# Transposing three units early, storing u in the output, and moving the weight-part stores to SyncE in a fused attention and MLP-mixer kernel

## The chip, the cores and the metric

The kernel runs on one core of one Trainium2 chip. The metric is device time in microseconds (us), the median of several runs; lower is better. Besides, one execution was taken by the hardware profiler; all durations of single instructions come from it. The engines are PE (TensorE, matrix products), DVE (VectorE), ACT (ScalarE), POOL (GpSimd) and SP (SyncE, which here only issues DMA transfers).

## The reference

All in float32. Eight batches of 576 tokens, 8 heads of 64, model width 512. First linear attention with a normalisation, then a token mixing (over the 576 tokens), then a channel mixing (over the 512 columns, hidden width 1536):

```python
kv = np.einsum('bhsd,bhse->bhde', k, v)
out = np.einsum('bhsd,bhde->bhse', q, kv)
rms = np.sqrt(np.mean(out * out, axis=-1, keepdims=True) + 1e-06)
x = out / rms * g_norm                      # then (B,H,S,D) -> (B, S, H*D)
h = np.maximum(x.transpose(0, 2, 1) @ w_tok1, 0.0) @ w_tok2
u = x + h.transpose(0, 2, 1)
h2 = np.maximum(u @ w_ch1, 0.0) @ w_ch2
return u + h2
```

## The kernel before

**First pass (0 to about 195 us).** Batches go in four pairs. For each pair `attention` computes kv, the attention output, its norm and x, and `token_mixing` turns x into u. The work of a pair's mixing is interleaved with the attention of the next pair by lists of step names that `play` reads word by word (`start`, `middle`, `steady`, `last`). Each name is a closure: "h00" a product of token mixing, "u3" the second product of tile 3, "g", "q", "t" parts of the norm, "f3" a load of a raw block of channel weights, a number so many steps of rounding those weights. x and u share the tiles `X[pair, i]`; two sets of them (`xps`) take turns, so that pair 2 overwrites pair 0. `tok2` stores u in DRAM from POOL's queue (lines 565 to 569).

**Units.** The channel mixing sees u as nine units of 512 tokens: unit b is the first 512 tokens of batch b, unit 8 collects the last 64 tokens of all eight batches. Each unit has a DRAM tile `u_dram[u]` (line 108). Unit 0 is group 0; the rest are groups 1 to 4 of two units, 1024 tokens (`units`, line 579).

**Transposing.** The channel mixing needs u with columns on partitions. `fetch_t(u, i)` loads 128 tokens (256 KB) into a buffer xt; `turn_blocks(u, i)` has DVE transpose blocks of 32 x 32 from xt into a buffer y (two instructions), and after each second tile issues four DMAs that write y to a DRAM tile `blocks_dram`. `fetch_half`, through `fetch_once` and `fetch_u`, loads these blocks into uT in full transposed order. All those DMAs are in SP's queue, which issues in program order.

**Products by Strassen-like schemes.** Both products of the channel mixing are done with seven block products in place of eight, at two levels (outer blocks o, inner parts n), so sums of weight blocks, of u and of v are needed. The sums of the weights are made once: `split(weight, o)` makes one outer block's parts and stores seven of them in DRAM (`parts_dram`). Parts of the first weight are stored by SP (`queue`, line 285), and two of the sums are made on POOL; parts of the second weight are stored by ACT's queue (`nc.scalar`), with DVE making all sums. Each split has five stores for the second weight, 35 for seven blocks. In `second` weight's case the sums lie in free halves of v tiles.

**The stage of group 0 (about 195 to 297 us).** `channel1_once` and `channel2_once` give the seven products of group 0 with whole weights in SBUF; `weave` distributes a list of other steps between them: sums (`firsts`, `lasts`), `parts1`, `parts2`, the loads and transposes of units 1 and 2 (`turn_unit`), the loads of uT of group 1 and of its first weight parts (lines 1299 to 1325).

**The groups 1 to 4 (from about 283 us, 138 us a group).** `channel1(g, n0)` and `channel2(g, n0)` put their products on numbered places, seven to an outer block, 49 to a layer; `put(place, step)` puts any other step behind the product of that place. A last loop emits products and steps place by place. A place takes PE about 1.34 us. `fetch_ahead` loads weight parts one block ahead; lines 980 to 985 place the transposes of the next group's units at places 2, 5, 9, 12, 49, 52, 76 and 80 with the load of each next tile one place behind; xt and y have one buffer each there (lines 1311, 1312). `outer_u` and `inner_u` make sums of u: the sum of block 4 takes, at place 10 of each group, one of three buffers "us". These buffers also hold results of the previous group's channel2, which POOL adds into the output with accumulating DMAs (`join`, line 1090); before that SP has copied u from `u_dram` to the output inside DRAM (line 1096). Group 4 instead has u in SBUF (`xg`, loaded by `fetch_x`), adds results there with DVE (`xadd`) and stores from it. Lines 1077 to 1086 place the sums of v (`ins`, `S1` to `S4`) in channel2.

Of the kernel before, what the change touches and what calls it, by code (L numbers as in the profile page):

```python
# [20 lines left out]
def kernel(  # L21
# [32 lines left out]
    nc = tc.nc  # L54
# [52 lines left out]
    kvp = [inp.tile([P, HP, P], F32, name=f"kvp{i}") for i in range(2)]  # L107
    u_dram = [dram.tile([J * P, DM], F32, name=f"u_dram{g}") for g in range(NU)]

# [8 lines left out]
    def dma(o, i, engine=nc.sync):  # L118
        keep(engine.dma_start(o, i))  # L119
# [160 lines left out]
    def split(weight, o):  # L280
# [3 lines left out]
        to = parts_dram[weight, o]  # L284
        queue, other = (nc.sync, nc.gpsimd) if weight == 1 else (nc.scalar, nc.vector)

# [230 lines left out]
    def token_mixing(pair, seeds, aside=()):  # L517
# [26 lines left out]
        def tok2(i):  # L544
# [19 lines left out]
            if i == 8:  # L564
                dma(u_dram[B][ts(pair, P)], x, nc.gpsimd)
            elif i % 2 == 1:
                dma(
                    u_dram[2 * pair + i // J][ds((i % J - 1) * P, 2 * P)]
                    .rearrange("(t p) e -> p t e", p=P), X[pair, i // 2], nc.gpsimd)
# [12 lines left out]
    def fetch_x(g, i):  # L582

        if g < NG:
            if i == 0:
                xg[g] = (late["xg"].tile([P, 2 * J, DM], F32, name="xg") if g else
                         late["xg0"].tile([P, J, DM], F32, name="xg"))
            dma(xg[g][:, ts(i, J)], u_dram[units(g)[i]].rearrange("(t p) e -> p t e", p=P))

    def fetch_t(u, i):  # L590

        if u < NU:
            xt[u, i] = late["xt"].tile([P, DM], F32, name="xt")
            dma(xt[u, i], u_dram[u][ts(i, P)])

    Q = 32
    blocks, blocks_dram = {}, {}

    def turn_blocks(u, i):
        if u >= NU:  # L600
            return
        half, n = i // 2, 2 * (i % 2)
        if n == 0:
            blocks[u] = late["y"].tile([P, NC, 2, NC, Q], F32, name="y")
        for o in range(2):
            keep(nc.vector.transpose(  # L606
                blocks[u][:, :, o, n:n + 2].rearrange("p b n t -> p n b t"),
                xt[u, i][:, ts(o, DH)].rearrange("p (n b t) -> p n b t", n=2, b=NC)))
        if n:
            t = blocks_dram[u, half] = dram.tile([NC, Q, NC, 2 * P], F32, name=f"blocks{u}{half}")  # L610
            for a in range(NC):
                dma(t[:, :, a].rearrange("b i x -> i b x"),
                    blocks[u][ds(a * Q, Q)].rearrange("p b o n t -> p b (o n t)"))

# [319 lines left out]
    def channel1(g, n0):  # L934
# [40 lines left out]
        for t, *places in ((2, None, 24, 28, 26), (7, 45, 46, 47, 48), (1, None, 44, 47, 46)):  # L975
            for place, (i, j) in zip(places, ((0, 0), (0, 1), (1, 0), (1, 1))):
                if place is None:
                    continue
                rectify(place, t, i, j)
        for k, place in enumerate((2, 5, 9, 12, 49, 52, 76, 80)):  # L980
            u = units(g + 1)[k // J]
            put(b + place, do(turn_blocks, u, k % J))
            if k < 7:
                put(b + place + 1, do(fetch_t, units(g + 1)[(k + 1) // J], (k + 1) % J))
        put(b + 84, do(fetch_t, units(g + 2)[0], 0))
        for place, step in zip((-2, 1, -1, 10), outer_u(g)):
# [3 lines left out]
    def channel2(g, n0):  # L990
# [86 lines left out]
        for place, steps in (  # L1077
                (-3, [ins[1][0]]), (-1, [ins[1][1]]), (1, [ins[1][3]]), (2, [ins[1][2]]),
                (3, [ins[2][0]]), (5, [ins[2][1]]), (6, [ins[4][0]]), (7, [ins[2][2]]),
                (8, [A[0]]), (9, [A[1]]), (10, [ins[2][3]]), (11, [S3[0]]), (12, [S3[1]]),  # L1080
                (13, [ins[4][1]]), (14, [ins[4][2]]), (15, [S2[0]]), (16, [ins[4][3]]), (17, [ins[7][0]]), (18, [xadd(0, 0, 1)] if g == NG - 1 else []),
                (19, [ins[7][1]]), (21, [S2[1], ins[7][2]]), (23, [ins[7][3]]), (24, [S1[0]]),
                (25, [ins[6][0]]), (29, [S4[0]]), (27, [ins[6][1]]), (28, [S1[1]]), (30, [ins[6][2]]),
                (31, [ins[5][0], ins[6][3]]), (33, [ins[5][1]]), (34, [xadd(0, 0, 2)] if g == NG - 1 else []),
                (35, [ins[5][2]]), (36, [S4[1]]), (37, [ins[5][3]]), (39, [ins[3][0]]), (41, [ins[3][1]]),
                (43, [ins[3][2]]), (45, [ins[3][3]])):
            put(b + place, *steps)

        if g < NG - 1:
# [4 lines left out]

            for i in range(2):
                put(b - 6 + 3 * i, do(lambda i: dma(out[units(g)[i], :LO], u_dram[units(g)[i]]), i))
            for place, step in ((12, join(0, 0, 1)), (20, join(0, 0, 2)), (26, join(1, 0, 4)), (40, join(0, 1, 6)),
# [6 lines left out]
        else:  # L1104
            for place, steps in ((36, [do(store_part, 0, 0, J, 0)]),
                                 (40, [xadd(1, 0, 4)]), (43, [xadd(0, 1, 6)]), (44, [radd(7, 6)]),
                                 (45, [xadd(1, 0, 7)]), (45, [xadd(0, 1, 5)]), (46, [xadd(1, 1, 7)]),
                                 (47, [xadd(1, 1, 5), do(store, g, 1)]),
                                 (48, [do(store_part, 0, 0, 2, 1)]), (49, [do(store_part, 0, 2, 4, 1)])):
                put(b + place, *steps)  # L1110
# [82 lines left out]
    for block in tok1[2:] + tok2:  # L1193
# [19 lines left out]
    steady = [[  # L1213
        "kv00 kv01 e00 e01 1 -d40 f3", "h00 1", "h01 1 f4", "a0 q00 g01 q01 g00 l00 1",
        "h10 t00 t01 1", "h11 l01 1", "hr 1 z2 f5 f6", "a1 q10 g11 q11 g10", "kv10 kv11 e10 e11 t10 t11 m0 r0",
        "u0 i0 1", "u1 1 d00 l10", "u2 s01 z4 1 f7", "a2 q20 g21 q21 g20", "u3 s10 t20 t21",
        "u4 z6 1 l11", "a4 q40 g41 q41 g40 lq0", "u5 d11 t40 t41 1", "a3 q30 g31 q31 g30 lq1",
        "u6 t30 t31 m2 r2 i2 d20 p21 s30", "u7 1 d31 1", "u8 1"], [
        "kv00 kv01 e00 e01 1 -d40 f8", "h00 1", "h01 1 f9", "a0 q00 g01 q01 g00",
        "h10 t00 t01 1", "h11 1", "hr 1 z2 f10", "a1 q10 g11 q11 g10", "kv10 kv11 e10 e11 t10 t11 m0 r0",  # L1220
        "u0 i0 1", "u1 1 d00 f11", "u2 s01 z4 1", "a2 q20 g21 q21 g20", "u3 s10 t20 t21",
# [8 lines left out]
    more = {f"w{n}{k}": f for n, b in enumerate(tok1 + tok2) for k, f in enumerate(b)}  # L1230
    more |= {f"f{n}": b[0] for n, b in enumerate(channel)}
    rounding = stream(channel)

# [18 lines left out]
    late["u0"] = pool("u0", 1, "left", once)  # L1252
    late["xt"] = pool("xt0", 2, "left", once)
    late["y"] = pool("y0", 2, "left", once)
    fetch_t(0, 0)
    fetch_t(0, 1)
    fill = [list(rounding), mix_ch1()]
    woven = fill[0][:4] + fill[1] + fill[0][4:]

    def turn(i):  # L1260
        turn_blocks(0, i)
        if i + 2 < J:
            fetch_t(0, i + 2)
        if i % 2:
            fetch_once(i // 2)

    last = [
        "h00 c0 2 -d40 2", "h01 c1 2", "h10 c2 2", "h11 c3 2", "hr z2 1", "u0 z3 1", "u1 z4 1", "u2 z5",
        "u3 z6 1", "u4 z7 1", "u5 z8 1", "u6 1", "u7 c4", "u8"]
    more = {f"c{i}": do(turn, i) for i in range(J)}  # L1270
    more[f"c{J}"] = lambda: [f() for f in t_sums(lambda n: uT[0][:, SB[n]])]
    woven = iter(woven)
# [7 lines left out]
    late["xg0"] = pool("xg0", 1, "right", w2s)  # L1280
    late["sv0"] = pool("sva", 2, "right", tail)
    late["r0"] = pool("r0", 5, "right", tail)
# [4 lines left out]
    firsts, lasts = mix_ch2()  # L1287
    parts1 = [f for o in ORDER1 for f in split(1, o)]
    parts2 = [f for o in ORDER2 for f in split(2, o)]

    def turn_unit(u):
        steps = [do(fetch_t, u, 0)]
        for i in range(J):
            steps.append(do(turn_blocks, u, i))
            if i + 1 < J:
                steps.append(do(fetch_t, u, i + 1))
        return steps

    fill, turns = firsts + parts1, turn_unit(1)
    for i, f in enumerate(turns):  # L1300
        fill.insert(5 * i, f)
    weave(channel1_once(0), fill)
    tail.close()
# [6 lines left out]
    late["ui"] = pool("ui", 2)  # L1310
    late["xt"] = pool("xt", 1)
    late["y"] = pool("y", 1)
    late["tmp"] = pool("tmp", 1)
    late["us"] = pool("us", 3)
    turns = turn_unit(2)
    waits = [[do(fetch_u, 1, 0, h) for h in range(2)]] + [[f] for f in lasts[:2]] + [turns[:1]] + [[f] for f in lasts[2:]]
    for i in range(J):
        waits += [turns[2 * i + 1:2 * i + 3]] + [[f] for f in parts2[2 * i:2 * i + 2]]
        if i < 2:
            waits += [[do(fetch_w, 0, 2 * i), do(fetch_w, 0, 2 * i + 1)]]  # L1320
    waits += [[f] for f in parts2[8:16]] + [[do(fetch_u, 1, 1, 0), do(fetch_w, 1, 0)]]
    waits += [[f] for f in inner_u(1, 1)] + [[do(fetch_u, 1, 1, 1), do(fetch_w, 1, 1)]]
    waits += [[f] for f in parts2[16:]] + [[do(fetch_t, units(2)[0], 0)]] + [[f] for f in outer_u(1)[:1]]
    waits += [[lambda: staged[-1]()], outer_u(1)[2:3]]
# [57 lines left out]
```

## Time and profile before

| What | Value |
|---|---|
| median of 3 runs | 861.64 us (861.49 to 863.35) |
| the profiled execution, whole | 857.33 us |
| its span, first to last instruction | 855.5 us |
| mean granted PE clock | 0.973 |
| DMA moved | 205.22 MB, mean 240 GB/s |
| SP's queue (q1) | 103840 packets, 169.31 MB |
| POOL's queue (q0) | 16880 packets, 23.60 MB |
| ACT's queue (q10) | 12096 packets, 11.37 MB |
| xt loads | 36 of 256 KB, median 4.1 us from issue to landing |
| block writes (y to blocks) | 72 of 128 KB, median 2.5 us |
| transposes on DVE | 72, mean 422 ns |
| accumulating stores | 27 of 512 KB, median 9.9 us (from r) and 8.1 us (from us) |

A profile line that begins with a start and a duration is one instruction, or a merged run of equal ones (x12: twelve records; one product of the program leaves two). What stands in brackets at its end is the idle time of the engine before it and what ended it. SPq and ACTq are DMA issues. "PE ps_d <- ACT ps_d" in a list of waits reads: PE, about to write ps_d, waited for ACT's last work on it.

### The profile page before, as it was taken

How to read it: one execution, taken by the hardware profiler on the slowest of the kernel's cores; microseconds unless marked ns; L12 is line 12 of the kernel's file. 1: busy time of each engine (PE TensorE's matmuls, PEld its weight loads, DVE VectorE, ACT ScalarE, POOL GpSimd, SP SyncE). 2: the span in 40 equal slices, each digit the busy share in tenths (PEclk: the TensorE clock that was granted, in tenths of full speed). 3: DMA queues.
4: the chain of work that ended last, by engine and by line, in shares of the span. 5: the costliest groups of instructions: out<-in, count | busy, mean ns of one | idle time of the engine just before them, and what ended most of it. 6: DMA issues, size and time to landing. Idle time of an engine off the chain costs nothing.

```text
span 855.5 us, 14847 instructions
## 1 busy us (share of the span) xinstructions
PE 792.4 (93%) x5832; PEld 661.3 (77%) x5832; DVE 609.9 (71%) x901; ACT 265.2 (31%) x513; POOL 79.2 (9%) x86
## 2 busy tenths in 40 slices
PE   6999999999994499999998999998999999899995
PEld 6655545447883388899987899897889998789995
DVE  3667585996756558988647889755898863788885
ACT  2366474842100033421132252022342113224110
POOL 1302020202500000001210001020000121000000
PEclk9999999999997799999999999999999999999997
DMA  9999994566998976789897589799679899655542
GB/s 303 315 342 334 343 377 152 195 211 201 345 287 271 381 219 189 245 248 248 219 249 229 148 281 293 210 226 253 188 248 258 235 223 277 206 149 154 143 126 74
DMA packets 132884, 205.22 MB, mean 240 GB/s; under 512 B 9712, under 2 KB 89584, under 8 KB 132720
## 3 DMA queue, kind: packets, MB, share of 16 engines
q1 hardware_dynamic: 103840, 169.31, 62.4%
q0 software_dynamic: 16880, 23.60, 13.9%
q10 hardware_dynamic: 12096, 11.37, 4.1%
q8 instruction: 46, 0.75, 0.4%
q14 instruction: 22, 0.18, 0.1%
HBM read 148.80 MB, written 61.73 MB: 246 GB/s over the span
## 4 chain that ended last, share of the span: by engine, by line
PE 66%; DMA 14%; DVE 11%; issue 4%; ACT 3%; SPq 2%; POOL 1%; DVEq 0%; ACTq 0%; POOLq 0%
PE ps_d L131 21%; PE ps_b L131 13%; PE ps_a L131 13%; PE ps_h L131 7%; DMA xt<-u_dram 7%; PE ps_u L131 6%; DVE v L122 3%; PE ps_kv L131 2%; SPq L119 2%; PE ps_o L131 2%; DMA out_dram<-r 2%; DVE sv L122 2%; PE ps_c L131 1%; DVE y L606 1%; ACT x L486 1%
## 5 line engine op out<-in xcount | busy, mean ns | idle before, releaser
L131 PE MATMUL ps_d<-ui,w 128*128 128x256 f32 x504 | 124.9, 394 | 16.3 <-ACT ps_d L128 11.9
L131 PEld LDWEIGHTS ps_d<-ui,w 128*128 128x128 f32 x504 | 98.6, 198 | 32.8 <-ACT ps_d L128 12.3
L128 ACT COPY ps_d<-ps_a 128x768 f32<-128x768 f32 (+1 forms) x56 | 32.0, 571 | 247.2 <-PE ps_a L131 190.4
L122 DVE TENSOR_TENSOR v<-v,v 128x1536 f32<-128x1536 f32 (+2 forms) x70 | 103.0, 1476 | 0.3
L131 PE MATMUL ps_b<-w,sv 128*128 128x128 f32 x672 | 87.4, 281 | 7.6 <-DVE sv L122 7.6
L131 PEld LDWEIGHTS ps_b<-w,sv 128*128 128x128 f32 x672 | 81.8, 197 | 8.6 <-DVE sv L122 8.4
L131 PE MATMUL ps_a<-w,v 128*128 128x128 f32 x672 | 84.2, 275 | 0.0
L131 PEld LDWEIGHTS ps_a<-w,v 128*128 128x128 f32 x672 | 79.9, 192 | 0.2
L131 PE MATMUL ps_d<-w,v 128*128 128x128 f32 x528 | 67.6, 279 | 2.7 <-DVE xg L122 2.7
L131 PE MATMUL ps_u<-h,w_tok 128*128 128x512 f32 (+1 forms) x160 | 67.5, 607 | 0.2
L131 PEld LDWEIGHTS ps_d<-w,v 128*128 128x128 f32 x528 | 64.2, 196 | 3.0 <-DVE xg L122 2.9
L606 DVE STREAM_TRANSPOSE y<-xt 128x256 f32<-128x256 f32 x72 | 27.6, 422 | 53.6 <-DMA xt<-u_dram 52.6
L131 PE MATMUL ps_h<-x,w_tok 128*128 128x512 f32 (+1 forms) x160 | 65.5, 603 | 0.2 <-ACT x L486 0.2
L125 ACT ACTIVATE v<-v 128x768 f32<-128x768 f32 (+1 forms) x54 | 42.6, 822 | 68.3 <-DVE v L122 65.9
L131 PE MATMUL ps_d<-w,sv 128*128 128x128 f32 x480 | 60.1, 275 | 0.0
L131 PEld LDWEIGHTS ps_d<-w,sv 128*128 128x128 f32 x480 | 57.1, 192 | 0.2
L1092 POOL DMA_DIRECT2D out_dram<-us x12 | 15.4, 1281 | 386.6 <-ACT us L128 278.4
L131 PEld LDWEIGHTS ps_h<-x,w_tok 128*128 128x128 f32 (+1 forms) x160 | 26.1, 189 | 32.2 <-issue 27.7
L131 PEld LDWEIGHTS ps_u<-h,w_tok 128*128 128x128 f32 (+1 forms) x160 | 24.7, 179 | 31.3 <-issue 25.4
L131 PE MATMUL ps_a<-uT,w 128*128 128x256 f32 x192 | 47.5, 384 | 0.4
L131 PE MATMUL ps_b<-ui,w 128*128 128x256 f32 x168 | 41.9, 386 | 6.3 <-DVE v L122 6.3
L432 DVE TENSOR_TENSOR x<-ps_o,g_sb 128x512 f32<-128x512 f32 x32 | 21.5, 687 | 33.8 <-PE ps_o L131 29.2
(141 smaller groups left out, 1224.0 us busy)
## 6 DMA issues: line engine op xcount, KB each, us to landing
w<-parts SPq DMA_DIRECT2D x168, 384.0 KB, 4.1
w<-parts SPq DMA_DIRECT2D x56, 192.0 KB, 3.6
qT<-in_q_dram SPq DMA_DIRECT2D x8, 1152.0 KB, 9.2
xt<-u_dram SPq DMA_DIRECT2D x36, 256.0 KB, 4.1
blocks<-y SPq DMA_DIRECT2D x72, 128.0 KB, 2.5
uT<-blocks SPq DMA_DIRECT2D x36, 256.0 KB, 5.6
k_in<-in_k_dram SPq DMA_DIRECT2D x16, 512.0 KB, 9.0
u_dram<-x POOLq DMA_DIRECT2D x16, 512.0 KB, 5.7
```

The lines of the kernel that those rows point to most:

```text
L119: keep(engine.dma_start(o, i))
L122: keep(engine.tensor_tensor(out=o, in0=a, in1=b, op=op))
L125: keep(nc.scalar.activation(o, a, AF.Relu))
L128: keep(nc.scalar.copy(o, a))
L131: keep(nc.tensor.matmul(*a, **kw))
L432: keep(nc.vector.tensor_mul(x, bank[c, h], g_sb.to_broadcast([P, number(c), D])))
L486: keep(nc.scalar.activation(x[:, k, h], x[:, k, h], AF.Copy, scale=inv[:, k, h]))
L606: keep(nc.vector.transpose(blocks[u][:, :, o, n:n + 2].rearrange("p b n t -> p n b t"), xt[u, i][:, ts(o, DH)].rearrange("p (n b t) -> p n ...
L1092: return lambda: keep(nc.gpsimd.dma_start(out[u, :LO, ts(j, DH)].rearrange("(t p) e -> p t e", p=P), rs[o][0], accum_op=ALU.add))
```

## The change

It has six parts.

1. Units 0, 1 and 2 are transposed in the first pass, right from X, by `turn_early` at the names "x00" to "x21" in the two `steady` lists. The space for y is a part of `w_ch2` that has not been filled yet. No xt load is needed. The list `last` loses its transposes ("c0" to "c3" are now sums of u) and gets the first five steps of `parts1` ("s0" to "s4"); the pool for these sums has four buffers, not two.
2. In `split` the second weight's parts are stored by SP.
3. u is stored in the output itself; only unit 8 has a DRAM tile of its own, `u_rest`. The six copies inside DRAM go.
4. In the groups the transposes are at places 2, 6, 10, 14, 17, 20, 23 and 26; xt has two buffers, and loads run two tiles ahead, the first two of the next group's at places 60 and 66.
5. In channel2 the order of the sums for blocks 6 and 5 is changed at places 30 to 38.
6. In group 4 the additions into xg are at other places, mostly earlier.

PE's instructions and their order are the same. DVE's stream has the same instructions in another order. ACT's stream loses 35 DMA issues.

```diff
-    u_dram = [dram.tile([J * P, DM], F32, name=f"u_dram{g}") for g in range(NU)]
+    u_rest = dram.tile([J * P, DM], F32, name="u_rest")
+    u_rows = lambda u: u_rest if u == B else out[u, :LO]
...
-        queue, other = (nc.sync, nc.gpsimd) if weight == 1 else (nc.scalar, nc.vector)
+        queue, other = (nc.sync, nc.gpsimd if weight == 1 else nc.vector)
...
-                    u_dram[2 * pair + i // J][ds((i % J - 1) * P, 2 * P)]
+                    u_rows(2 * pair + i // J)[ds((i % J - 1) * P, 2 * P)]
...
+    def turn_tile(y, x, i):
+        for o in range(2):
+            keep(nc.vector.transpose(
+                y[:, :, o, 2 * i:2 * i + 2].rearrange("p b n t -> p n b t"),
+                x[:, ts(o, DH)].rearrange("p (n b t) -> p n b t", n=2, b=NC)))
+
+    def put_blocks(u, half, y):
+        t = blocks_dram[u, half] = dram.tile([NC, Q, NC, 2 * P], F32, name=f"blocks{u}{half}")
+        for a in range(NC):
+            dma(t[:, :, a].rearrange("b i x -> i b x"),
+                y[ds(a * Q, Q)].rearrange("p b o n t -> p b (o n t)"))
...
+    def turn_early(u, half):
+        pair, c = u // 2, 2 * (u % 2) + half
+        y = w_ch2[:, c if pair == 0 else 2 + c, :NC].rearrange("p b (o n t) -> p b o n t", o=2, n=NC)
+        for i in range(2):
+            turn_tile(y, X[pair, c][:, i], i)
+        put_blocks(u, half, y)
...
-        for k, place in enumerate((2, 5, 9, 12, 49, 52, 76, 80)):
+        for k, place in enumerate((2, 6, 10, 14, 17, 20, 23, 26)):
             u = units(g + 1)[k // J]
             put(b + place, do(turn_blocks, u, k % J))
-            if k < 7:
-                put(b + place + 1, do(fetch_t, units(g + 1)[(k + 1) // J], (k + 1) % J))
-        put(b + 84, do(fetch_t, units(g + 2)[0], 0))
+            if k < 6:
+                put(b + place, do(fetch_t, units(g + 1)[(k + 2) // J], (k + 2) % J))
+        for i in range(2):
+            put(b + 60 + 6 * i, do(fetch_t, units(g + 2)[0], i))
...
-                (25, [ins[6][0]]), (29, [S4[0]]), (27, [ins[6][1]]), (28, [S1[1]]), (30, [ins[6][2]]),
-                (31, [ins[5][0], ins[6][3]]), (33, [ins[5][1]]), (34, [xadd(0, 0, 2)] if g == NG - 1 else []),
-                (35, [ins[5][2]]), (36, [S4[1]]), (37, [ins[5][3]]), (39, [ins[3][0]]), (41, [ins[3][1]]),
+                (25, [ins[6][0]]), (29, [S4[0]]), (27, [ins[6][1]]), (28, [S1[1]]), (30, [ins[6][3]]),
+                (31, [ins[5][0]]), (32, [ins[6][2]]), (33, [ins[5][1]]), (34, [xadd(0, 0, 2)] if g == NG - 1 else []),
+                (35, [ins[5][2]]), (36, [ins[5][3]]), (38, [S4[1]]), (39, [ins[3][0]]), (41, [ins[3][1]]),
...
-            for i in range(2):
-                put(b - 6 + 3 * i, do(lambda i: dma(out[units(g)[i], :LO], u_dram[units(g)[i]]), i))
...
-                                 (40, [xadd(1, 0, 4)]), (43, [xadd(0, 1, 6)]), (44, [radd(7, 6)]),
-                                 (45, [xadd(1, 0, 7)]), (45, [xadd(0, 1, 5)]), (46, [xadd(1, 1, 7)]),
-                                 (47, [xadd(1, 1, 5), do(store, g, 1)]),
+                                 (27, [xadd(1, 0, 4)]), (38, [xadd(0, 1, 6)]), (39, [radd(7, 6)]),
+                                 (40, [xadd(1, 0, 7)]), (41, [xadd(1, 1, 7)]), (45, [xadd(0, 1, 5)]),
+                                 (46, [xadd(1, 1, 5), do(store, g, 1)]),
...
-    fill, turns = firsts + parts1, turn_unit(1)
-    for i, f in enumerate(turns):
-        fill.insert(5 * i, f)
-    weave(channel1_once(0), fill)
+    weave(channel1_once(0), firsts + parts1[5:])
...
-    late["xt"] = pool("xt", 1)
+    late["xt"] = pool("xt", 2)
...
+    waits = [[do(fetch_u, 1, 0, h) for h in range(2)]] + [[f] for f in lasts]
+    waits += [[f] for f in parts2[:4]] + [[do(fetch_u, 1, 1, h) for h in range(2)]] + [[f] for f in parts2[4:8]]
+    waits += [[do(fetch_w, 0, k) for k in range(4)]] + [[f] for f in parts2[8:16]]
+    waits += [[f] for f in inner_u(1, 1)] + [[do(fetch_w, 1, k) for k in range(2)]]
+    waits += [[f] for f in outer_u(1)[:1]] + [[f] for f in parts2[16:]]
+    waits += [[do(fetch_t, units(2)[0], i) for i in range(2)]]
```

## The prediction

> **What bounds the kernel now.** I read the page's first two parts, then the busy windows by stage, then the waits of the tensor engine, then the timelines of each engine around the long waits.
>
> The page says that the tensor engine (PE) is the bound on average, and the slices say where it is not: slices 11 and 13, and the end.
>
> ```profile
> PE 792.4 (93%) x5832; PEld 661.3 (77%) x5832; DVE 609.9 (71%) x901; ACT 265.2 (31%) x513; POOL 79.2 (9%) x86
> PE   6999999999994499999998999998999999899995
> PEclk9999999999997799999999999999999999999997
> ```
>
> The windows put a number on it. Columns: busy us of PE, weight loads, DVE, ACT, POOL, then clock, DMA share, GB/s.
>
> ```profile
> 240.00:270.00 30.00, 19.56 (x91) 16.88 (x89) 12.33 (x25) 0.00 (x0) 0.00 (x0) 0.89 0.88 269
> 270.00:297.00 27.00, 14.61 (x60) 12.30 (x60) 19.64 (x36) 0.67 (x1) 0.00 (x0) 0.82 1.06 354
> ```
>
> PE is idle about 23 us of these 57, at a lowered clock. The waits of PE, longest first, give the rest:
>
> ```profile
> PE ps_d L131 <- ACT ps_d L128: 11.9, 1, 11.9
> PE ps_c L131 <- DVE us L122: 11.1, 1, 11.1
> PE ps_b L131 <- DVE sv L122: 7.6, 4, 2.1
> PE ps_b L131 <- DVE v L122: 6.3, 3, 3.4
> PE ps_d L131 <- DVE v L122: 4.4, 4, 2.0
> PE ps_d L131 <- DVE xg L122: 2.7, 1, 2.7
> ```
>
> Who held the releasers is on their own timelines. DVE (start, duration, work, idle before it):
>
> ```profile
> 250.81 0.77 DVE L606 STREAM_TRANSPOSE y<-xt 128x256 f32<-128x256 f32 x2 [7.06 <-DMA xt<-u_dram]
> 264.43 0.77 DVE L606 STREAM_TRANSPOSE y<-xt 128x256 f32<-128x256 f32 x2 [6.65 <-DMA xt<-u_dram]
> ...
> 727.39 1.23 DVE L122 TENSOR_TENSOR us<-uT,us 128x1024 f32<-128x1024 f32 x1 [6.81 <-DMA out_dram<-us]
> ```
>
> So the 11.1 us wait is DVE standing in order behind transposes whose input (xt) was still loading. ACT:
>
> ```profile
> 290.88 5.35 ACTq L119 DMA_DIRECT2D parts<-v  x4
> 296.33 0.78 ACT L128 COPY ps_d<-ps_a 128x768 f32<-128x768 f32 x1 [56.81 <-DMA xt<-u_dram]
> ```
>
> From 238.96 to 296.23 us ACT issues 35 stores of weight parts, and the copy that PE needs stands behind them in its queue: that is the 11.9 us wait.
>
> **What the Trainium skill says.** "TensorE: Matmul & The Clock Gate", Part 1, states two clocks, half and full, the half one after an idle window of about 3.4 us. The trace agrees that a gap costs more than itself (after the 2.06 us gap at 404.51 the next 12 instructions took 2.92 us instead of 1.50), though gaps of 1.4 us left no trace: at 821.51 the same 12 took 1.60. "DMA: Bandwidth & Descriptors", section "Issuing engines are not separate DMA queues", says that transfers of SP, ACT and POOL share the same 16 engines, so that a second issuer saves only issue time. The trace fits: with both issuing, 270 to 297 us stands at a DMA share of 1.06. I use it to expect that moving the stores to SP doesn't move more bytes.
>
> **Part 1: three units transposed in the first pass.** Units 0 to 2 have 12 xt loads of 256 KB, 24 transposes and 24 block writes of 128 KB. The loads go. The transposes (422 ns mean, 10.1 us) read x in SBUF and move to 80 to 165 us, where DVE is busy 58.86 of 84.8 us and PE waits for DVE nowhere; DVE has 26 us idle there, so I price them at 0 (up to 2, if one gain lands late; nothing below 0). Their 24 writes (3.1 MB) stand in SP's queue before loads of k, v and raw weights; 79.7 to 121.7 us has a DMA share of 1.06 but 121.7 to 164.5 only 0.58, and the loads passed over (k_in issued at 84.95) serve products at about 121.7 us: covered.
> What goes is the 11.09 us gap at 259.56, and the half clock after it (6.84 against 5.34 us for 24 instructions: 1.5). 12.6 us.
>
> **Part 2: weight parts stored by SyncE.** ACT loses its 35 issues, so the 11.90 us gap at 285.26 goes with its slow restart (2.93 and 1.92 against 1.46 each for 6 instructions: 1.9). 13.8 us.
> What is late next: SP now holds everything in one line. The stage's seven products take 7 x 5.34 = 37.4 us from 233.3, so group 1 starts at about 271. After the 35 stores' bulk come the first two xt loads of unit 3, and DVE reaches their transpose three products into group 1 (about 273). Bytes ahead of or beside them: 7 x 1344 KB of parts, 8 x 256 KB of uT, 2.1 MB of w, 1 MB of output, 0.5 MB of xt, less the last 0.8 MB: about 14.7 MB. At 354 GB/s, the best of this stage, 41.5 us from 239: 280; at 309 (17.6 MB in these 57 us) 47.6: 286. SP must also let the last output store wait for DVE at about 271.5, then issue 5 stores at 0.5 to 1.1 us. I put the landing at 281 to 283. PE can run 7 products (9.3 us, to 280) before it needs a PSUM bank that DVE, standing at that transpose, has not read; DVE then needs 2.1 us more. A new gap of 4 us plus 1.7 of half clock: 5.7. Bounds: 0 (landing before 278) to 12.
>
> **Part 3: u in the output itself.** Six copies of 1 MB inside DRAM go (12 MB of traffic in groups 1 to 3). PE has no gap at their place (351.5 and later): 0 directly. The accumulating stores of POOL keep their order and their releasers.
>
> **Part 4: steady groups, transposes at places 2 to 26 with two xt buffers.** Between groups PE loses now: 1.29 and 2.77 (441, 451), 1.96 and 0.44 (581, 595), 3.40 (726), with about 1.7 of half clock each time: 14.9 in all. The first two are behind xt. The third has no transpose in it: DVE waits for the last accumulating store (issued 717.62, landed 727.37) to release a us buffer. The same store is issued at 441.55 and 580.94, 11.8 and 11.3 us after its group's first product against 11.1, so when xt is early, this wait stands there instead: three gaps of 4.0, 3.6 and 3.4 plus 1.7 each = 16.1. Net -1.2 (a loss); bounds from a gain of 6 (a quieter DMA lets these stores land 3 us earlier each time) to a loss of 4. The 0.73 gap in group 1 goes into part 2's. Eight transpose pairs (6.2 us) in places 2 to 26 find about 3 us of DVE idle behind the resume, and the second half of channel1 has more: 0, at worst 3 a group.
>
> **Part 5: sums of v reordered.** The gaps 2.06, 2.06, 2.06 (404, 544, 682) with 1.6 of half clock each: the sv that PE needs now comes ahead of v, u and sv work of 0.87 + 0.34 + 0.69 (a transpose, gone) + 0.87 = 2.8 us. The third part of that order then comes about 0.4 late, too short to lower the clock. 3 x (3.66 - 0.4) = 9.8 us. The fourth (1.42, last group) also gets an addition of 1.15 us ahead of it: 0.
>
> **Part 6: the end.** Additions into xg move into 3.4 us of DVE idle (832.6, 837.0), so the 2.66 us gap at 843.38 goes and its slow last product gains about 0.4: 3.0.
>
> Sum: 12.6 + 13.8 - 5.7 - 1.2 + 0.7 + 9.8 + 3.0 = 33.0 us. From the span of 855.5 that is 822.5; the profiled execution took 857.33 (1.8 around the span), so 824.3. The median of the runs shown is 861.64, 4.3 above the profiled one: 861.64 - 33.0 = 828.6, and I say **828.5 us**.
>
> **Rivals.**
> Everything hides (20%): xt lands in time and the accumulating stores are earlier, so 5.7 and some 6 more come back: about 816. For it: DMA loses 15 MB in all. Against it: group 3's end shows the store wait without xt.
> The single line of SP is worse (17%): 35 stores at about 1.1 us each as ACT had them are 39 us beside some 25 us of uT, w, output and xt issues, so the backlog reaches into group 1 and its w loads come late too: 10 to 16 us more, about 841. For it: share 1.06 already. Against: group 1's first w and uT are issued ahead of most stores.
> Slower (9%): y has one buffer. In places 14 to 26 a half's block writes have only 3 places (4.0 us) until the next transpose overwrites y, while four issues take 1.8 us and land in 2.5. If SP issues them late behind w loads waiting for their buffers, DVE stalls three times a group in the stretch where it has least idle. It decides from about 4.2 us a stall beyond DVE's slack: 9 stalls x 4.2 = 38, more than the 33 gained. At 5 us it gives 861.6 - 33 + 45 = 874.
> That nothing comes of it, the waits all replaced (1%): 861. My forecast has 53%.
>
> **The numbers.** What a measurement here can tell from no change is about 0.2%, 1.7 us. Faster holds forecast, first two rivals and part of none: 0.90; same 0.01; slower 0.09. The range runs from 813 to 845: it takes the first two rivals in and part 2's bounds, and leaves out the slower case and the far ends.
>
> **What would show it.** Right: no PE gap at ps_c, ACT without DMA issues, a PE gap of some us eight products into group 1 behind a transpose waiting for xt; at each of the three group changes DVE's us<-uT,us waiting for out_dram<-us; no gap above 1 us before ps_b from sv in groups 1 to 3; PE's last product about 3 us nearer the end. Wrong: w<-parts or uT as releasers in the B stage, transposes waiting for block writes, or gaps in the first pass.

## The result and the profile after

The median of the changed kernel is 829.86 us (827.58 to 835.93, 4 runs) against 861.57 us (4 runs) of the kernel before on the same chip: ratio 0.964, 95% interval 0.9584 to 0.9696. The profiled execution took 827.58 us with a span of 825.8 us (before: 857.33 and 855.5), at a mean PE clock of 0.990 (0.973). Slow executions, more than 1.5% above the fastest of their kernel (one of e1's took 1164.01 us, one of the kernel before 899.61 us), are left out of all medians and ratios here.

The page of the changed kernel: busy time of the engines, then PE and its clock in 40 slices.

```profile
PE 784.8 (95%) x5832; PEld 657.4 (80%) x5832; DVE 607.9 (74%) x901; ACT 265.6 (32%) x513; POOL 78.8 (10%) x86
...
PE   6999999999999799999979999997999998999996
...
PEclk9999999999999999999999999999999999999999
```

Counted from 1, the hole before lay in slices 13 and 14 (the prediction names 11 and 13); it is closed but for a 7 in slice 14. Two more 7s (slices 21 and 28) stand a little after groups 2 and 3 begin. The windows of the changed kernel over the two stretches shown of before:

```profile
240.00:270.00 30.00, 30.00 (x141) 26.41 (x140) 20.29 (x39) 0.00 (x0) 0.00 (x0) 1.00 1.03 343
270.00:297.00 27.00, 21.61 (x93) 18.46 (x92) 15.38 (x28) 7.94 (x10) 0.00 (x0) 0.94 0.98 332
```

PE was busy 34.17 of these 57 us before, now 51.61. The waits of PE in the changed kernel (total, times, longest):

```profile
PE ps_b L132 <- DVE v L123: 18.0, 4, 5.4
...
PE ps_a L132 <- DVE v L123: 2.2, 3, 0.7
PE ps_d L132 <- DVE v L123: 1.6, 4, 0.8
PE ps_d L132 <- DVE xg L123: 1.0, 1, 1.0
```

The 11.9 us behind ACT and the 11.1 us at ps_c are gone. Most of what is left after the first pass, 18.0 of 23.2 us, stands in one line: four waits for v, a sum of DVE. The timeline of DVE in the changed kernel shows what held it at the first and the second of them:

```profile
281.68 0.77 DVE L602 STREAM_TRANSPOSE y<-xt 128x256 f32<-128x256 f32 x2 [7.00 <-DMA xt<-out_dram]
282.37 0.38 DVE L123 TENSOR_TENSOR ui<-us,ui 128x256 f32<-128x256 f32 x1
282.67 0.94 DVE L123 TENSOR_TENSOR v<-ps_b,u 128x768 f32<-128x768 f32 x1
...
422.72 0.77 DVE L602 STREAM_TRANSPOSE y<-xt 128x256 f32<-128x256 f32 x2 [2.90 <-DMA blocks<-y]
427.62 1.23 DVE L123 TENSOR_TENSOR us<-uT,us 128x1024 f32<-128x1024 f32 x1 [4.12 <-DMA out_dram<-us]
```

At 281.68 a transpose waits for its tile of unit 3 and the v that PE needs stands behind it. At 427.62, and again in groups 3 and 4, the sum of block 4 waits for a us buffer that the last accumulating store still reads.

A table by stage, from the PE timelines. A stage begins with its first product; "channel 1" runs from the first product of a group to the first one of its second layer. Differences in us, with what the prediction put there:

| Stage | before | after | difference | predicted |
|---|---|---|---|---|
| up to the second layer of group 0 | 233.50 | 232.80 | -0.70 | 0 |
| second layer of group 0 | 49.00 | 36.26 | -12.74 | -12.6 |
| group 1, channel 1 | 77.48 | 70.49 | -6.99 | -8.8 (-13.8 + 5.7 - 0.7) |
| groups 1, 2, 3, channel 2 | 69.76, 69.61, 67.98 | 66.19 each | -8.78 | -9.8 |
| groups 2, 3, 4, channel 1 | 70.25, 68.92, 69.22 | 70.86, 70.25, 70.25 | +2.97 | +1.2 |
| group 4, channel 2, and the end | 79.78 | 76.32 | -3.46 | -3.0 |
| span | 855.5 | 825.8 | -29.7 | -33.0 |

The table looks like a confirmation line by line. The experiments show that one line of it, channel 1 of group 1, is right for a wrong reason.

### The profile page after: what moved, and what is told of

The parts are those of the page before. It is cut to its first block, busy times and chain, and to the rows that moved or that the text cites. A ratio compares the mean times of both kernels' runs of the same rounds, so it can differ in the third digit from the quotient of the medians.

```text
span 825.8 us, 14832 instructions
## 1 busy us (share of the span) xinstructions
PE 784.8 (95%) x5832; PEld 657.4 (80%) x5832; DVE 607.9 (74%) x901; ACT 265.6 (32%) x513; POOL 78.8 (10%) x86
## 4 chain that ended last, share of the span: by engine, by line
PE 73%; DMA 11%; DVE 8%; issue 3%; ACT 2%; SPq 1%; POOL 1%; DVEq 0%; POOLq 0%; ACTq 0%
PE ps_d L132 21%; PE ps_b L132 13%; PE ps_a L132 12%; PE ps_h L132 7%; PE ps_u L132 7%; DMA out_dram<-r 6%; PE ps_v L132 4%; DMA out_dram<-us 4%; DVE v L123 3%; PE ps_c L132 3%; PE ps_kv L132 2%; PE ps_o L132 2%; PE ps_w L132 2%; ACT x L487 1%; DVE sv L123 1%
## 5 line engine op out<-in xcount | busy, mean ns | idle before, releaser
L132 PE MATMUL ps_d<-ui,w 128*128 128x256 f32 x504 | 121.5, 386 | 0.0
L132 PE MATMUL ps_b<-w,sv 128*128 128x128 f32 x672 | 84.4, 275 | 0.4 <-DVE sv L123 0.4
L132 PEld LDWEIGHTS ps_b<-w,sv 128*128 128x128 f32 x672 | 79.5, 192 | 0.5 <-DVE sv L123 0.5
L132 PE MATMUL ps_b<-ui,w 128*128 128x256 f32 x168 | 45.2, 409 | 18.0 <-DVE v L123 18.0
L132 PEld LDWEIGHTS ps_b<-ui,w 128*128 128x128 f32 x168 | 33.6, 202 | 24.4 <-DVE v L123 19.6
L132 PEld LDWEIGHTS ps_a<-uT,w 128*128 128x128 f32 x192 | 35.9, 190 | 8.5 <-DVE v L123 3.9
```

Source lines behind the costliest of these rows:

```text
L132: keep(nc.tensor.matmul(*a, **kw))
```

## The experiments

Times are medians; each ratio is to the kernel before, run on the same chip in the same series (860.27 us for e1 to e4, 861.43 for e5 to e8, 861.64 for e9 and e10, 861.09 for e11). e2, e3, e5, e7, e8 and e9 have two runs each; waits and stages are read from one profiled execution of each kernel.

### e1: part 2 alone

```diff
-        queue, other = (nc.sync, nc.gpsimd) if weight == 1 else (nc.scalar, nc.vector)
+        queue, other = (nc.sync, nc.gpsimd if weight == 1 else nc.vector)
```

> The kernel before with part 2 alone: second-weight parts stored by SyncE. Theory (one line for two jobs): the xt loads of unit 2 now stand behind those stores, DVE stands behind xt, so the gap before ps_c stays or grows past 11 us while the 11.9 us gap before ps_d changes its releaser from ACT to DVE or a DMA; the span stays within 6 us of 855.5. Rival (independent gaps, as in the sum of the prediction): the 11.9 us gap and its slow restart go alone, span about 842.

860.64 us (7 runs), ratio 0.9999 (0.9968 to 1.0031). The waits of PE in e1:

```profile
PE ps_b L131 <- DVE v L122: 19.2, 3, 12.4
PE ps_c L131 <- DVE us L122: 7.9, 1, 7.9
```

ACT's 11.9 us wait is gone, as it must be without its issues, and nothing is won: 12.4 us stand behind DVE instead, five products later (the eighth of group 1, not the third). The wait at ps_c did not stay or grow, as the theory had it, but shrank from 11.1 to 7.9 us. The transposes of e1 tell why PE waits for DVE: the xt loads now stand in SP's line behind the stores, and one keeps DVE waiting for 11.61 us. (Timeline of DVE in e1.)

```profile
260.57 0.77 DVE L606 STREAM_TRANSPOSE y<-xt 128x256 f32<-128x256 f32 x2 [6.11 <-DMA xt<-u_dram]
...
300.37 0.77 DVE L606 STREAM_TRANSPOSE y<-xt 128x256 f32<-128x256 f32 x2 [11.61 <-DMA xt<-u_dram]
```

### e2 and e3: parts 1 and 3, without and with part 2

e2 takes over the early transposes, the new lists and u in the output; ACT still stores, the groups stay as they were. xt has one buffer, so that only one tile is fetched ahead:

```diff
+    more |= {f"x{u}{half}": do(turn_early, u, half) for u in range(3) for half in range(2)}
...
-    weave(channel1_once(0), fill)
+    weave(channel1_once(0), firsts + parts1[5:])
...
+    waits += [[do(fetch_t, units(2)[0], 0)]]
```

> The kernel before with parts 1 and 3: three units transposed in the first pass, u in the output, ACT still stores the second weight's parts, groups as before. Theory: the gap before ps_c goes (12.6 us with its slow restart), group 1's first product comes at about 270, but ACT's 35 issues take until at least 280, so PE waits 10 to 15 us for the copy to ps_d: span 841 to 846. Rival (ACT was late only because DVE's sums were late): the gap before ps_d goes too, span 830 to 835.

839.56 us, ratio 0.976 (0.9677 to 0.9843). The theory fell: PE waits for ACT only 4.1 us, not 10 to 15; the rival, no wait at all, came closer. Waits of PE in e2:

```profile
PE ps_b L132 <- DVE v L123: 8.6, 2, 4.7
PE ps_b L132 <- DVE sv L123: 7.6, 4, 2.1
...
PE ps_d L132 <- ACT ps_d L129: 4.1, 1, 4.1
```

And ACT's own timeline in e2, with all its 35 stores still in it:

```profile
271.17 3.82 ACTq L120 DMA_DIRECT2D parts<-v  x4
275.08 0.78 ACT L129 COPY ps_d<-ps_a 128x768 f32<-128x768 f32 x1 [36.35 <-DMA parts<-v]
```

Before, the same copy ran at 296.33. ACT can issue the store of a sum only when DVE has made it. DVE ended its last sum at 271.92 us here (285.39 before), because it no longer stood behind transposes of units 1 and 2. That is only a part of the 21.2 us by which ACT ends its issues earlier, at 274.99 and not at 296.23. From the first issue to the last one, ACT before had 13.1 us of pauses and 44.1 us of issues; in e2 it has 3.1 us of pauses and 33.7 us of issues for the same 35 stores. The two longest pauses before, 4.42 and 5.25 us, are those in which DVE waited for xt (until 250.81 and 264.43). So about 10 us went because DVE was on time, and about 10 us because each issue took less time. Why the issues got shorter is not shown; the xt loads and block writes that left this stretch are a candidate.

e3 is e2 with the line of e1.

> The kernel before with parts 1, 2 and 3; groups, sums of v and the end as before. Theory: both gaps of the stage go and the new one behind xt of unit 3 comes (3 to 6 us, eight products into group 1): span 833 to 838, group 1's first product at 269 to 271. Rival (parts 1 and 2 only move the wait): first product of group 1 after 276, span above 843.

842.15 us, ratio 0.979 (0.9759 to 0.9821). The span, 840.7 us, lies above the theory's 833 to 838, but group 1's first product, at 269.66, and PE's gap of 4.20 us behind xt came as it said. Part 2 on top of part 1 wins nothing: channel 1 of group 1 takes 73.26 us against 71.17 in e2. ACT's wait is gone, and xt comes later: DVE waits for it 5.82, 4.05 and 1.54 us at the start of group 1 (3.72, 0.70 and 2.63 us in e2).

### e4: part 3 alone

```diff
-    u_dram = [dram.tile([J * P, DM], F32, name=f"u_dram{g}") for g in range(NU)]
+    u_rest = dram.tile([J * P, DM], F32, name="u_rest")
+    u_rows = lambda u: u_rest if u == B else out[u, :LO]
...
-            for i in range(2):
-                put(b - 6 + 3 * i, do(lambda i: dma(out[units(g)[i], :LO], u_dram[units(g)[i]]), i))
```

> The kernel before with part 3 alone: u stored in the output, no copies inside DRAM. Theory: PE has no gap at the copies' place, so the span stays within 2 us of 855.5 and the us release at the last group change stays at a gap of about 3.4. Rival (the copies' 12 MB slow the accumulating stores and loads): the three gaps at the group changes become 1 to 3 us shorter each, span 847 to 852.

860.90 us (17 runs), ratio 0.9997 (0.997 to 1.0025). Six copies of 1 MB fewer change nothing that can be measured.

### e5: part 5 alone

```diff
-                (25, [ins[6][0]]), (29, [S4[0]]), (27, [ins[6][1]]), (28, [S1[1]]), (30, [ins[6][2]]),
-                (31, [ins[5][0], ins[6][3]]), (33, [ins[5][1]]), (34, [xadd(0, 0, 2)] if g == NG - 1 else []),
-                (35, [ins[5][2]]), (36, [S4[1]]), (37, [ins[5][3]]), (39, [ins[3][0]]), (41, [ins[3][1]]),
+                (25, [ins[6][0]]), (29, [S4[0]]), (27, [ins[6][1]]), (28, [S1[1]]), (30, [ins[6][3]]),
+                (31, [ins[5][0]]), (32, [ins[6][2]]), (33, [ins[5][1]]), (34, [xadd(0, 0, 2)] if g == NG - 1 else []),
+                (35, [ins[5][2]]), (36, [ins[5][3]]), (38, [S4[1]]), (39, [ins[3][0]]), (41, [ins[3][1]]),
```

> The kernel before with part 5 alone (order of the sums of v). Theory (the prediction's): the three gaps of 2.06 us before ps_b from sv, at 404, 544 and 682, and the half clock after them go, and nothing late replaces them by more than 0.4: channel2 of groups 1 to 3 takes 66 to 67 us each instead of 69.76, 69.61 and 67.98; span 8 to 10 us less than 855.5, so about 846; time about 851. Rival: the sums only change which of them is late (the third part of the order, or v in the next wait), channel2 stays at 68 to 70 us and the time within 3 us of before.

853.75 us, ratio 0.9904 (0.9867 to 0.9941): 7.7 us by the medians. Channel 2 of groups 1 to 3 took 66.85, 66.85 and 66.86 us, as the theory said; the sv gaps are gone. Gaps of 0.94 us behind v stand in their place (408, 544, 683), where the theory allowed 0.4: at 406.40 DVE still has a transpose of 0.7 us ahead of that v, which part 4 takes away. The span of the profiled execution, 852.3 us, is only 3.2 less than before, since its channel 1 of group 3 took 72.02 us (68.92) and the second layer of group 0 took 51.31 (49.00), both behind waits that the edit doesn't touch.

### e6: the changed kernel without part 2

```diff
-        queue, other = (nc.sync, nc.gpsimd if weight == 1 else nc.vector)
+        queue, other = (nc.sync, nc.gpsimd) if weight == 1 else (nc.scalar, nc.vector)
```

> The changed kernel with part 2 undone: the 35 stores of second-weight parts are back on ACT, all else as changed. Theory (formed after the first four runs): ACT was late only because DVE's sums were late behind xt, so with part 1 in place part 2 gains nothing; ACT ends its issues by about 275, PE has a gap of about 4 us before ps_d in place of the 5.4 us gap before ps_b, xt lands earlier; group 1's channel1 takes 68 to 71 us (70.5 in the changed kernel); time 825 to 831. Rival (the prediction's term for part 2): ACT's line still costs some 12 us, channel1 of group 1 takes 80 us or more; time 838 to 843.

832.45 us, ratio 0.9684 (0.9625 to 0.9743), which overlaps the changed kernel's interval. Channel 1 of group 1: 69.77 us (70.49). The waits of PE in e6:

```profile
PE ps_b L132 <- DVE v L123: 13.8, 3, 5.2
...
PE ps_d L132 <- ACT ps_d L129: 3.9, 1, 3.9
```

One of the four waits for v has become a wait of 3.9 us for ACT. The theory's stage held; the time lies 1.5 us above its range. The rival, 12 us for ACT's line, fell.

### e7: block 3's results in another pool

Seven us buffers are taken in a group, from a pool of three: results of blocks 1, 2, 6 and 3, then sums of blocks 5, 6 and 4. The last sum therefore takes the buffer of block 3's results, whose store is the last one issued. With block 3 in the pool r the sum takes block 6's, whose store is issued at place 40, 14 places before block 3's.

```diff
-                    name = "us" if o in (1, 2, 6, 3) else "r"
+                    name = "us" if o in (1, 2, 6) else "r"
```

> The changed kernel with one edit: the results of channel2's block 3 lie in the pool r and not in us, so that the sum of block 4 at place 10 of the next group no longer waits for the last accumulating store. The computation is the same. Theory: the three gaps of 4.38, 3.78 and 4.43 us before ps_b, with 1.7 us of half clock each, go: 17.7 us, channel1 of groups 2 to 4 takes about 65 us each instead of 70.86, 70.25 and 70.25; time about 812. Rival: behind that wait stands the next one, a transpose waiting for the writes of y (2.9 us at the first group change) or for xt, so that 2 us of gap remain each time with the half clock: time 820 to 824.

812.25 us, ratio 0.9422 (0.9388 to 0.9457): 17.6 us less than the changed kernel. Channel 1 of groups 2 to 4: 65.30, 65.15 and 63.86 us. The waits of PE in e7:

```profile
PE ps_b L132 <- DVE v L123: 6.2, 3, 5.4
PE ps_a L132 <- DVE v L123: 2.4, 3, 0.9
```

Of 18.0 us behind v, little more than group 1's start is left. The rival's wait came, but small: at 424.66 DVE waits 3.26 us for the writes of y, and PE loses 0.51 us. No other wait took the place of the three.

### e8: xt of unit 3 earlier

```diff
     waits += [[do(fetch_w, 0, k) for k in range(4)]] + [[f] for f in parts2[8:16]]
+    waits += [[do(fetch_t, units(2)[0], i) for i in range(2)]]
...
-    waits += [[do(fetch_t, units(2)[0], i) for i in range(2)]]
```

> The changed kernel with one edit: the first two xt loads of unit 3 stand in SP's line behind the loads of group 1's first weight parts, eight split steps and the u sums earlier than before. Theory: xt lands before DVE needs it, the gap of 5.38 us at 278.3 and 1.7 us of half clock go, channel1 of group 1 takes 63 to 65 us instead of 70.49; time about 823. Rival: the DMA engines are full there (share 1.01), so the same bytes are late elsewhere (weight parts or uT of group 1): a gap of 4 us or more stays in the stage; time 827 to 831.

837.75 us, ratio 0.9718 (0.9682 to 0.9754): no faster than the changed kernel (the intervals overlap), and outside what either theory said. Timeline of DVE in e8:

```profile
276.58 0.76 DVE L602 STREAM_TRANSPOSE y<-xt 128x256 f32<-128x256 f32 x2
...
279.43 0.76 DVE L602 STREAM_TRANSPOSE y<-xt 128x256 f32<-128x256 f32 x2
...
291.43 0.77 DVE L602 STREAM_TRANSPOSE y<-xt 128x256 f32<-128x256 f32 x2 [8.11 <-DMA blocks<-y]
```

xt was there when the first two transposes came up. The third must overwrite y, and y's four writes, issued by SP at 283.21 to 285.39 behind loads of w, landed at 291.4. PE waits 5.32 us at 288.91 in place of 5.38 at 278.29; channel 1 of group 1 takes 70.38 us (70.49). The 8 us more of this profile lie in the three later group changes, where the waits of PE were 6.51, 5.65 and 6.75 us instead of 4.38, 3.78 and 4.43. The edit does not touch these; in e6, whose edit does not either, they were 5.20, 4.85 and 3.78. Why the stores landed later is not settled.

### e9: e8 with the transposes further apart

```diff
-        for k, place in enumerate((2, 6, 10, 14, 17, 20, 23, 26)):
+        for k, place in enumerate((2, 6, 14, 18, 26, 30, 36, 40)):
```

> The kernel of e8 (xt of unit 3 loaded early) with the transposes of every group at places 2, 6, 14, 18, 26, 30, 36 and 40, so that the four writes of y have eight places (10.7 us) before the next transpose overwrites it. Theory: what took xt's place in e8 was the single buffer y, whose writes stand in SP's line and landed at 291.4 while DVE waited 8.11 us; so now the gap of 5.32 us at 288.9 goes with its half clock, channel1 of group 1 takes 62 to 65 us (70.38 in e8), and DVE's waits for blocks<-y sum to under 2 us (13.1). Time about 823 to 829, since the three waits for the last accumulating store stay at 4 to 7 us each. Rival: the DMA engines are simply full there, a gap of 4 us or more stays in channel1 of group 1, for weight parts, uT or xt; time as e8, 835 to 839.

822.9 us, ratio 0.9549 (0.9454 to 0.9645). Channel 1 of group 1 takes 63.08 us, and the 0.75 us gaps of all groups are gone as well. The waits of PE in e9 that are left in the groups' first layers:

```profile
PE ps_b L132 <- DVE v L123: 10.9, 3, 4.3
```

These are the three group changes (3.36, 3.21, 4.33 us). So the bytes were not the limit at group 1's start: the order in SP's line and y's one buffer were. The writes of y landed no earlier (the third transpose ran at 291.29, in e8 at 291.43), but it no longer stood ahead of sums that PE needed. The gaps of 0.75 us were not waits for y at all. In the changed kernel DVE had a transpose, without any wait, in a full stretch just ahead of a v (timeline of DVE in the changed kernel; the same at 438.57 and 575.01):

```profile
299.86 1.75 DVE L123 TENSOR_TENSOR v<-v,v 128x1536 f32<-128x1536 f32 x1
301.53 0.76 DVE L602 STREAM_TRANSPOSE y<-xt 128x256 f32<-128x256 f32 x2
302.21 0.92 DVE L123 TENSOR_TENSOR v<-ps_a,v 128x768 f32<-128x768 f32 x1
```

### e10: e7 and e9 together

> e9 and e7 together: xt early, transposes spread, block 3's results in r. Theory: the three waits are separate, so their gains add: from e7's 812.25, about 7 us of group 1's start and 2.2 us of the three gaps of 0.75 us with no new wait: 802 to 805, each channel1 62 to 65 us. Rival: the transposes at places 30 to 40 meet DVE where it is busy 12.3 of 13 us (459 to 472 in e7), so that sums of v come late for channel2 and gaps of 1 to 3 us arise at the end of each channel1: 808 to 814.

802.77 us (801.91 to 804.89, 4 runs), ratio 0.9324 (0.9256 to 0.9392): better than both kernels, 27 us below the changed one. The four layers of channel 1 take 63.38, 64.09, 64.08 and 63.86 us. PE's slices and clock on the page of e10:

```profile
PE   6999999999999999999999999999999999999996
...
PEclk9999999999999999999999999999999999999999
```

After 200 us PE has four gaps of 0.3 us or more left, the longest 0.96 us, and 3.7 us of idle time in all by the timeline.

### e11: e10 without part 2

The edit is that of e6.

> e10 with part 2 undone (second-weight parts stored by ACT again). It asks what part 2 is worth once the wait that it brought is gone. Theory: DVE's sums end at about 273 in both, so ACT ends its issues at about 275 and PE waits 3.9 us before ps_d, as in e2 and e6, with 1.7 us of half clock: channel1 of group 1 takes 67 to 69 us instead of 63.38; time 807 to 810. Rival: with SP freed of 35 issues everything in the stage comes earlier, and ACT's lateness costs 2 us or less: 801 to 805.

811.94 us (810.48 to 813.16, 4 runs), ratio 0.9428 (0.9383 to 0.9472). Against e10 that is 9.2 us by the medians; the single times lie apart, the two intervals just touch. Channel 1 of group 1 takes 72.90 us instead of 63.38; all other stages from group 0's second layer on are the same to 0.01 us. ACT's timeline in e11:

```profile
274.95 5.61 ACTq L120 DMA_DIRECT2D parts<-v  x4
280.65 0.78 ACT L129 COPY ps_d<-ps_a 128x768 f32<-128x768 f32 x1 [39.55 <-DMA parts<-v]
```

The theory's mechanism is right and its size was too small: PE's wait is 7.3 us, not 3.9. The last four issues took 5.61 us here and 3.70 in e6, and began 3.5 us after group 1's first product instead of 2.0. Why they took longer is open.

## Why the prediction was right, point by point

**The time.** 828.5 predicted, 829.86 measured. The span fell by 29.7 us, not by 33.0; that the medians agree more closely, to 1.4 us, is luck with runs that lie between 827.58 and 835.93. The sum came out because with parts 1 and 2 both in place the long gaps of group 0 and group 1 had to go, whichever part earned them. The total could not show that the split between the two parts was wrong.

**Part 1** was given 12.6 us, and the stage shows 12.74. But it does more: e2, with ACT's stores in place, also shortens channel 1 of group 1 by 6.3 us (77.48 to 71.17). Its span is 20.5 us less than before.

**Part 2** was given 13.8 us, because "ACT loses its 35 issues". This is the step that failed: it took the gap of 11.9 us to be the price of the issuer alone. The issues did hold ACT's copy until 296.23. But DVE was late to the same moment (timeline of DVE in the kernel before):

```profile
284.84 0.55 DVE L122 TENSOR_TENSOR v<-w_ch,v 128x384 f32<-128x384 f32 x1
...
296.35 0.77 DVE L606 STREAM_TRANSPOSE y<-xt 128x256 f32<-128x256 f32 x2 [6.57 <-DMA xt<-u_dram]
```

The first line is the last of its weight sums, the second the first transpose of group 1, which waited for xt. With ACT free PE met DVE instead (e1). And most of ACT's lateness went with part 1, the 35 stores still in place (e2): partly by shorter pauses, partly by shorter issues. The bracket of ACT's copy in the prediction names xt too, but proves nothing: the copy does not read xt, and ACT's last issue ended just then. Alone the part is worth nothing (e1), on top of part 1 channel 1 was about 2 us longer in one profile each (e3), in the changed kernel it is within the uncertainty (e6), and only once xt, y and the us buffer are out of the way is it worth 9 us (e11). The prediction read the two gaps of 11 us as two causes with one price each; xt in front of DVE was behind the first, and part 1, which removed it, also took most of the second (11.9 to 4.1 us in e2).

**The new wait of xt** was foreseen in its place and kind: landing at 281 to 283, measured 281.68; a gap of 4 us plus 1.7, measured 5.38 plus 1.7 (it began at 278.29, not at 280, since the products of group 0 follow each other every 5.18 us and not every 5.34). What is late next after it, y, the prediction had only in its slower case; e8 shows that it was ready to take over.

**Part 3** at 0: confirmed by e4.

**Part 4** was said to be a net loss of 1.2, three waits for the last accumulating store in place of five others. The waits came as named: 4.38, 3.78 and 4.43 us against 4.0, 3.6 and 3.4. e7 shows their price directly: 5.56, 5.10 and 6.39 us, 17.05 in all (predicted 16.1). DVE's own work on the transposes in places 2 to 26 was priced at 0, at worst 3 us a group; it cost PE 0.75 us in each of groups 1 to 3, gone in e9. In all channel 1 of groups 2 to 4 lost 2.97.

**Part 5** at 9.8, measured 8.78 in the changed kernel, where the transposes have left channel 2, and 7.7 by e5's medians. The mis-sized term is the half clock: 1.6 us were counted after all three gaps. In the profile of before the third has none (the 12 instructions after 682.90 took 1.60 us, those after 404.51 and 544.36 took 2.92 and 2.83).

**Part 6** at 3.0, measured 3.46, with the 1.42 us sv gap of group 4 among it, which shrank to 0.35 and a gap of 0.79 behind v.

**The slower rival.** The waits for the writes of y were real, 9.6 us of DVE in six of them, but no gap of PE in the changed kernel is theirs. In groups 2 and 3 the longest of them, 2.90 and 3.86 us, were followed by a wait for the us buffer that ended later still. They show once another wait is gone: 0.51 us of PE in e7, 5.32 us in e8.

The Trainium skill's "DMA: Bandwidth & Descriptors" says in "Issuing engines are not separate DMA queues" that issuing from several engines saves only the sequencer's time. The runs agree as far as the bytes go: with either issuer the DMA share in ten us at group 1's start is 1.04 with SP's stores (e10, from 272) and 1.04 with ACT's (e6, from 271). But what stands behind the issuer matters more than the issue: 9.5 us of channel 1 in e11, where it is a copy that PE needs.

## What to carry to other kernels

When two engines are late in the same stretch, look at what the second one's queue was waiting for before counting both gaps: an in-order queue that issues stores of another engine's results is at least as late as that engine. And check whether both are late to the same moment, since then removing one of them wins nothing. Before moving a load earlier, ask what the reader's next wait is; here it was the single buffer behind it, and moving the load alone won nothing (70.38 us of channel 1 against 70.49). In a pool that takes turns, the last buffer taken gets the last one released: count which store that is, since putting one tile into another pool was worth 17.6 us.

## What the runs showed of the hardware

The same gap of 2.06 us before the same product was followed by a slow stretch of PE in 5 of 15 cases (three groups each in before, e1, e2, e3 and e4): 12 instructions took 2.08 to 2.92 us in place of 1.60. In before and after, gaps of 1.47 us and less left no slow stretch, and those of 3.78 us and more all did; between them both happened (2.77 us did in before, 2.82 us in e1 did not). "TensorE: Matmul & The Clock Gate", Part 1, puts the change of the clock after an idle window of about 3.4 us; in these traces shorter gaps were enough in some cases, so a gap of 2.06 us costs, by an estimate from these cases, anything from 2.1 to 3.7 us. Timelines of PE, of before and then of e2:

```profile
406.57 2.92 PE L131 MATMUL ps_b<-w,sv 128*128 128x128 f32 x12 [2.06 <-DVE sv L122]
...
684.96 1.60 PE L131 MATMUL ps_b<-w,sv 128*128 128x128 f32 x12 [2.06 <-DVE sv L122]
```

```profile
525.78 1.60 PE L132 MATMUL ps_b<-w,sv 128*128 128x128 f32 x12 [2.06 <-DVE sv L123]
662.58 1.60 PE L132 MATMUL ps_b<-w,sv 128*128 128x128 f32 x12 [2.06 <-DVE sv L123]
```
